# Four row maxima in an attention kernel, taken by sign clearing and halving

## The chip, the cores and the metric

The kernel runs on one core of a Trainium2 chip. The metric is the device time of one execution in microseconds (us), as the median of several runs. A core has five engines that each work through an instruction list of their own: PE (TensorE, matrix products), ACT (ScalarE), DVE (VectorE), POOL (GpSimd) and SP (SyncE, which here only issues transfers). An engine takes its instructions strictly in order, and a semaphore wait at the head of a list holds all that is behind it.

## The reference

```python
x = A_x                                                       # (1, 2048, 512), bf16
g = sigmoid((x * gate_w).sum(-1, keepdims=True))
# a: attention, 32 heads of 16 channels
qkv = (x @ wqkv).reshape(B, S, 3, 32, 16).transpose(2, 0, 3, 1, 4)
p = softmax(einsum("bhqd,bhkd->bhqk", q, k) * 16 ** -0.5, axis=-1)
a = einsum("bhqk,bhkd->bhqd", p, v) ... @ wo
# b: a feed-forward block, F = 1792
b = (silu(x @ w_gate) * (x @ w_up)) @ w_down
return g * a + (1 - g) * b
```

The exponentials of the softmax are kept in range by a bound that needs, for each head and channel, the largest magnitude of the keys over all 2048 positions. That maximum is what the change computes in another way.

## The kernel before, in words

The attention is cut into 32 units (4 blocks of 512 queries by 8 groups of 4 heads), and a unit into 16 tiles of 128 keys. For each tile PE multiplies keys with queries into PSUM (tiles `s_t` and `d_t`). The `s_t` scores become exponentials on ACT (`e_t<-s_t`, 1024 columns for each instruction). The `d_t` scores are a share that ACT has no time for: DVE takes them out of PSUM with one multiply-add into a 16-bit pattern (`c_t<-d_t`), and from this pattern DVE and POOL make shifted copies (`c_t<-c_t`; in some tiles the home of the pattern is named `kaug` or `wd_t`), which PE sums up with the values (`o_ps<-c_t,vaug`), as it does with `e_t`.

The order of the work is settled while the kernel is built. A planner runs through the program with a price for each instruction, keeps the planned time of each engine, and writes one fixed order for every engine. The projections of keys, queries and values (`kp`, `qp`, `vp`) and the feed-forward block (`gu`, `dps`, `ops`) are put between the scores, in small pieces, and share three PSUM banks with the `d_t` tiles (`m_tile`, L396): a new tile goes into the bank whose old one DVE has copied out.

POOL gets part of the copies as strips of columns. `g_now` (L1063) looks at what DVE has queued next that is not "wide" (L340; the wide ones are the fast copies and products between SBUF tiles), and `strip` (L1021) cuts a strip for POOL that fits into just that time. `beside` (L1040) makes the strip wait for DVE's last wide instruction. DVE's eviction of a PSUM tile is not wide in this sense, and neither is the step that is changed here, which is entered with a planned cost of 2.46 us (`later(2.46, top, ...)`, L1529). The change leaves this entry, and so the planned order, as it was.

The step itself is `k_bound(b)` (L517), called four times, for b = 0 to 3. Its input `kst[b]` holds 128 rows (8 heads by 16 channels) of 2048 keys in bf16; it lies in the tile `on` for b = 0, 2 and 3 and in `bblk` for b = 1, so the four show in the profile as `kb<-on` and `kb<-bblk`. `kb` is a 128x4 column tile; `k_rows` (L520) uses its column later (`kbt<-on,kb`) and sends the result into `kaug` with eight transfers on the SP queue. `mt` (128 x 14 x 512) holds the feed-forward block's hidden values; its parts 10 to 13 (2048 columns) serve the first unit as scratch (L1345) and are free from then until the feed-forward block fills them. All DVE and POOL instructions go through one helper, so the profile gives line L206 for each of them; all matrix products have L194, all activations L197.

Of the kernel before, what the change touches and what calls it, by code (L numbers as in the profile page):

```python
# [9 lines left out]
ALU = mybir.AluOpType  # L10
AX = mybir.AxisListType
BF16 = mybir.dt.bfloat16
F32 = mybir.dt.float32
U16 = mybir.dt.uint16
# [94 lines left out]
def kernel(  # L109
# [15 lines left out]
    S, D = x.shape  # L125
# [82 lines left out]
    vec = Ordered(nc.vector)  # L208
# [23 lines left out]
    for c0 in (D, 0):  # L232
        queue.dma_start(out=wqk[:, :, c0 + 64:c0 + D],
                          in_=A_wqkv[:, c0 + 64:c0 + D].rearrange("(dc p) c -> p dc c", p=P))
# [18 lines left out]
    mt = big.tile([P, FC, QBW], BF16, name="mt")  # L253
# [54 lines left out]
    kb = const.tile([P, NB], F32, name="kb")  # L308
# [87 lines left out]
    def m_tile(name, ride=None):  # L396
        while m_ready() is None:
            stuck()
        i = min((i for i in range(3) if banks[i] is not None), key=lambda i: banks[i])
        if ride is None:  # L400
            plan.pe = max(plan.pe, banks[i])
        else:
            ride.append(max(plan.pe - ROUND, banks[i]) + ROUND)
            plan.pe = max(plan.pe, ride[0])
        banks[i] = None
        held[i] = ps_m[i].tile([P, QBW], F32, tag=f"m{i}", name=name)
        return held[i]
# [88 lines left out]
    kst = {}  # L496
# [18 lines left out]
                       lambda p: later(0.6, lambda: end(tb, p)))  # L515

    def k_bound(b):  # L517
        vec.tensor_reduce(out=kb[:, b:b + 1], in_=kst[b][:, :], axis=AX.X, op=ALU.max, apply_absolute_value=True)

    def k_rows(b):  # L520

# [69 lines left out]
    def q_pieces(qb, b):  # L591
        def landed(p):
            me = plan.chain
            later(0.6, lambda: end(p, me), key=("q", b))

        def rows(t, r):
            for hh in range(8):
                gg, j = hh // 4, hh % 4
                if (b, gg) != (0, 0):
                    queue.dma_start(out=get_q(qb, 2 * b + gg)[32 * j + r:32 * j + r + DH, j % 2, :],  # L600
                                      in_=t[DH * hh:DH * (hh + 1), :])

        def end(p, me):
            qst = work.tile([P, QBW], BF16, tag="qst", name="qst")
            vec.tensor_copy(out=qst[:, :], in_=p[:, :])
            m_free(p, plan.dve)
            rows(qst, 0)

            aq = work.tile([P, QBW], BF16, tag="aq", name="aq")

            def mag():
                vec.tensor_scalar(out=aq[:, :].bitcast(U16), in0=qst[:, :].bitcast(U16), scalar1=0x8000, scalar2=None,
                                  op0=ALU.bitwise_or)
                rows(aq, DH)
            plan.chain = me
            later(0.21, mag, plan.dve, ("q", b))
        return columns(DC, "qp", lambda dc: wqk[:, dc, P * b:P * (b + 1)],
                       lambda dc: xT[:, dc, qb * QBW:(qb + 1) * QBW], landed)
# [3 lines left out]
    def q0_pieces(qb):  # L622

        st = {}

        def landed(p):
            st["p"] = p
            later(0.6, mag, key=("aq", qb))
            later(0.21, clear, key=("aq", qb))

        def mag():
            vec.tensor_copy(out=mt[:, 5, :], in_=st["p"][:, :])

        def clear():
            vec.tensor_scalar(out=mt[:, 5, :].bitcast(U16), in0=mt[:, 5, :].bitcast(U16), scalar1=0x7FFF, scalar2=None,
                              op0=ALU.bitwise_and)
            st["at"] = plan.dve + 0.12

        def bound():
            bound_add(st["p"], kneg0, mt[:, 5, :])  # L640
            spend("C", 1, st["at"])
            variants(st["p"], q0[qb], work.tile([P, QBW], BF16, tag="qst", name="qst")[:, :], note=q0_notes.setdefault(qb, []))
        return (columns(DC, "qp", lambda dc: wpad[0][:, dc, :], lambda dc: xT[:, dc, qb * QBW:(qb + 1) * QBW], landed),
                [(1, bound, False)], lambda: st["at"] <= plan.pe)
# [646 lines left out]
    def last_rows(t):  # L1291
        cs = slice(t * P, (t + 1) * P)
        return lambda i: ((onc[QB - 1][:, i, cs], wo_t[:, i, :]) if i < NB - 1 else
                          (osbs[UNITS - 2][:, cs], wo_l[:, 0, :]) if i == NB - 1 else (ident[:, :], bblk[:, t, :]))
# [71 lines left out]
    for i0, i1, h in ((0, TQ, fore), (TQ, FT, aft)):  # L1366
        for dc in (DC - 1, DC - 2):
            spare_s = dc < DC - 1 and i0
            p = ps_s.tile([P, 2 * QBW], F32, tag="s", name="tp") if spare_s else m_tile("tp")
# [14 lines left out]
    for i, dc in [(0, dc) for dc in arrived[:3]] + [(1, dc) for dc in arrived] + [(0, arrived[3])]:  # L1384
        p, h = kps[i]
# [19 lines left out]
    for v in range(2):  # L1405
        for i, h in enumerate(halves):
            if i > v:
                act(out=q0a[:, v, h], in_=qps[i][:, 0:HQ], func=ACT.Copy, scale=vsel[:, v:v + 1])
            else:
                vec.tensor_scalar(out=q0a[:, v, h], in0=qps[i][:, 0:HQ], scalar1=vsel[:, v:v + 1], scalar2=None,  # L1410
                                  op0=ALU.mult)
# [92 lines left out]
    for qb in range(1, QB):  # L1504
        d = qb * KT
        q, bd, hold = q0_pieces(qb)
        q = pace.add(q, 0, d - 13, second)
# [4 lines left out]
    for qb in range(QB):  # L1512
        for b in range(NB):
            d = UNIT.index((qb, max(2 * b, 1))) * KT
            after = []
            if qb == 0:
                ks = []
                for tb in range(QB):
                    prev = [pace.add(k_pieces(b, tb), 0, d - 40 + tb, prev)]
                    ks += prev  # L1520

                def bnd(b=b):
                    me = plan.chain

                    def top():
                        k_bound(b)
                        plan.chain = me
                        later(0.21, lambda: k_rows(b), plan.dve, ("k", b))
                    later(2.46, top, key=("k", b))  # L1529
                after = prev = [pace.add([(0.2, bnd, False)], 0, d - 34, ks)]  # L1530

            if b == 0:
                rel = UNIT.index((qb - 1, 2)) * KT + 1 if qb else 0
            elif b == 1:
                rel = UNIT.index((qb - 1, 6)) * KT + 1 if qb else 0
            else:
                rel = UNIT.index((qb, 2 * b - 2)) * KT + 1 if (qb, b) != (0, 2) else UNIT.index((0, 2)) * KT + 1
            q = pace.add(q_pieces(qb, b), rel, d - QLEAD, after)
            need.setdefault(d - 12, []).append(q)
            for g in {max(2 * b, 1), 2 * b + 1}:  # L1540
                q_of[UNIT.index((qb, g))] = q
# [440 lines left out]
    while steps:  # L1982
# [14 lines left out]
        if rest and not (best and best[0] <= plan.pe) and (best is None or best[1] != ("v", 2 * KF - 1)) and max(plan.pe, al_at(rest[0][0])) + 0.12 <= min(lim, 1e8):  # L1997
# [3 lines left out]
            w, r = last_rows(tq)(i)  # L2001
# [55 lines left out]
```

## Time and profile before

| | |
|---|---|
| time before | 742.08 us, median of 3 runs (741.69 to 742.15) |
| profiled execution, its own time | 742.09 us |
| its span, first to last instruction | 740.4 us |
| busy time | PE 721.8, DVE 715.5, ACT 728.4, POOL 299.6 us |
| the four maxima (`kb<-on`, `kb<-bblk`) | 2270, 2276, 2270 and 2286 ns; starts 62.6, 93.6, 122.6 and 169.4 us |
| granted TensorE clock | 0.999 |

What lies around the span is 1.7 us. A row of the timeline gives start, duration, engine, line, operation, the tile written, the tiles read, and the shape; a release is shown in brackets where the engine sat idle before. A duration includes the time in which an instruction waits inside the engine, and an instruction can start a little before the one ahead of it has ended, so start-to-start distances say more than durations.

### The profile page before, as it was taken

Reading aid. Unit: us, or ns where it says so; the run is one execution under the profiler, and the core shown is the slowest. Engines: PE = TensorE matmul, PEld = TensorE weight load, DVE = VectorE, ACT = ScalarE, POOL = GpSimd, SP = SyncE. Lnnn points to the kernel's source line nnn. Section 1 sums busy time; section 2 is a strip of 40 time slices with the busy share of each in tenths; the row PEclk is TensorE's granted clock in tenths of the full one; section 3 lists DMA queues with packets and bytes.
Section 4 is the critical chain, followed back from the end, with each engine's and each line's share of the span. In section 5 each row is a group of like instructions: output and inputs, shape, how many; then the busy total and the mean of one; then the engine's idle time right before and its main releaser. Section 6 shows DMA issues by size and latency. Waiting matters only on the chain.

```text
span 740.4 us, 23142 instructions
## 1 busy us (share of the span) xinstructions
PE 721.8 (97%) x9296; PEld 213.6 (29%) x9296; DVE 715.5 (97%) x1223; ACT 728.4 (98%) x828; POOL 299.6 (40%) x370
## 2 busy tenths in 40 slices
PE   8999999999999999999999999999999999999997
PEld 3323222232222222322222222222222222222223
DVE  5999999999999999999999999999999999999995
ACT  7999999999999999999999999999999999999996
POOL 4044242234453336345444225544445255343441
PEclk9999999999999999999999999999999999999999
DMA  9001233355210012320200041302001231200001
GB/s 223 14 2 29 56 62 62 63 141 101 68 44 13 17 42 68 72 48 11 58 17 24 15 107 33 80 21 60 18 12 29 64 80 44 46 19 14 20 26 36
DMA packets 93523, 36.29 MB, mean 49 GB/s; under 512 B 76448, under 2 KB 92968, under 8 KB 93416
## 3 DMA queue, kind: packets, MB, share of 16 engines
q1 hardware_dynamic: 91688, 34.49, 20.0%
q8 instruction: 72, 1.18, 0.7%
q10 hardware_dynamic: 1728, 0.33, 0.2%
q14 instruction: 35, 0.29, 0.1%
HBM read 21.42 MB, written 2.35 MB: 32 GB/s over the span
## 4 chain that ended last, share of the span: by engine, by line
PE 59%; ACT 27%; issue 6%; DVE 6%; DMA 2%; ACTq 0%; DVEq 0%
ACT e_t L197 24%; PE s_t L194 21%; PE o_ps L194 17%; PE gu L194 7%; PE ops L194 6%; DVE c_t L206 3%; ACT th L197 2%; PE qp L194 2%; PE vp L194 2%; PE dps L194 1%; PE kp L194 1%; DVE mt L206 1%; DMA wqk<-in_A_wqkv_dram 1%; DVE kaug L206 1%; DMA rb<-in_A_wqkv_dram 1%
## 5 line engine op out<-in xcount | busy, mean ns | idle before, releaser
L197 ACT ACTIVATE e_t<-s_t 128x1024 bf16<-128x1024 f32 x754 | 704.1, 1098 | 0.6 <-PE s_t L194 0.2
L206 DVE TENSOR_SCALAR c_t<-d_t 128x512 uint16<-128x512 f32 x468 | 307.2, 681 | 3.4 <-PE d_t L194 2.7
L194 PE MATMUL s_t<-qx,kaug 32*128 32x512 bf16 (+2 forms) x1208 | 233.4, 383 | 9.6 <-ACT e_t L197 8.4
L206 POOL TENSOR_SCALAR c_t<-c_t 128x352 uint16<-128x352 uint16 (+19 forms) x210 | 149.0, 710 | 210.1 <-DVE c_t L206 141.5
L194 PEld LDWEIGHTS <-kaug 32*128 32x128 bf16 (+1 forms) x2056 | 80.6, 91 | 311.5 <-issue 308.3
L194 PE MATMUL d_t<-qx,kaug 32*128 32x512 bf16 x440 | 150.2, 384 | 0.0
L194 PE MATMUL o_ps<-e_t,vaug 128*32 128x512 bf16 (+2 forms) x1608 | 148.5, 372 | 0.0
L194 PE MATMUL o_ps<-c_t,vaug 128*32 128x512 bf16 (+2 forms) x1388 | 123.8, 372 | 0.2
L206 DVE TENSOR_SCALAR c_t<-c_t 128x2048 uint16<-128x2048 uint16 (+8 forms) x185 | 116.5, 641 | 0.5
L206 POOL TENSOR_TENSOR c_t<-c_t 128x480 bf16<-128x480 bf16 (+8 forms) x53 | 65.2, 1241 | 101.7 <-DVE c_t L206 69.9
L194 PEld LDWEIGHTS <-vaug 128*32 128x32 bf16 x3236 | 67.1, 95 | 104.7 <-issue 92.4
L194 PE MATMUL gu<-xT,wg 128*32 128x512 bf16 x896 | 72.1, 384 | 0.0
L194 PE MATMUL gu<-xT,wu 128*32 128x512 bf16 x896 | 66.5, 382 | 0.3 <-DVE kaug L206 0.2
L194 PE MATMUL ops<-wd_t,mt 128*32 128x512 bf16 x672 | 55.9, 382 | 0.0
L206 DVE TENSOR_TENSOR c_t<-c_t 128x1568 bf16<-128x1568 bf16 (+8 forms) x50 | 46.8, 937 | 0.0
L206 DVE SCALAR_TENSOR_TENSOR gs<-th,gu 128x512 bf16<-128x512 bf16 x56 | 38.0, 678 | 2.0 <-ACT th L197 1.9
L206 DVE TENSOR_SCALAR kaug<-d_t 128x512 uint16<-128x512 f32 x60 | 39.6, 682 | 0.0
L206 DVE SCALAR_TENSOR_TENSOR mt<-gs,gu 128x512 bf16<-128x512 bf16 x56 | 37.9, 677 | 0.5 <-PE gu L194 0.5
L197 ACT ACTIVATE th<-gu 128x512 bf16<-128x512 f32 x56 | 37.9, 677 | 0.0
L194 PE MATMUL s_t<-q,kaug 32*128 32x512 bf16 (+1 forms) x184 | 35.8, 385 | 1.0 <-ACT e_t L197 0.9
L194 PEld LDWEIGHTS <-mt 128*32 128x32 bf16 (+1 forms) x1058 | 24.6, 95 | 27.2 <-issue 21.4
L206 POOL TENSOR_SCALAR c_t<-kaug 128x1088 uint16<-128x1088 uint16 (+15 forms) x21 | 18.4, 875 | 26.0 <-DVE c_t L206 12.7
(151 smaller groups left out, 561.0 us busy)
## 6 DMA issues: line engine op xcount, KB each, us to landing
wg<-in_B_w_gate_dram SPq DMA_DIRECT2D x56, 128.0 KB
wu<-in_B_w_up_dram SPq DMA_DIRECT2D x56, 128.0 KB
on<-osb SPq DMA_DIRECT2D x120, 16.0 KB
rb<-rr SPq DMA_DIRECT2D x15, 128.0 KB
kaug<-kbt SPq DMA_DIRECT2D x28, 64.0 KB
wd_t<-in_B_w_down_dram SPq DMA_DIRECT2D x7, 256.0 KB
qx<-qst SPq DMA_DIRECT2D x96, 16.0 KB
qx<-aq SPq DMA_DIRECT2D x96, 16.0 KB
```

The costliest lines, as they stand in the source:

```text
L194: return ordered(nc.tensor.matmul(*args, **kw))
L197: ordered(nc.scalar.activation(*args, **kw))
L206: return lambda *a, **kw: ordered(f(*a, **kw))
```

## The change

Instead of one reduction with absolute value over 2048 columns, the new step clears the sign bits of all 2048 columns into `mt`'s parts 10 to 13, takes the maximum of the first half with the second three times (1024, 512 and 256 columns are left), and reduces the last 256 columns. It runs on DVE, at the same place in DVE's list. Each of the five instructions reads what the one ahead has written and waits for it by semaphore. The instruction lists of PE, ACT, POOL and SP are the same as before.

```diff
     def k_bound(b):
-        vec.tensor_reduce(out=kb[:, b:b + 1], in_=kst[b][:, :], axis=AX.X, op=ALU.max, apply_absolute_value=True)
+
+        m = mt[:, 10:14, :].rearrange("p a q -> p (a q)")
+        vec.tensor_scalar(out=m.bitcast(U16), in0=kst[b][:, :].bitcast(U16), scalar1=0x7FFF, scalar2=None,
+                          op0=ALU.bitwise_and)
+        for w in (S // 2, S // 4, S // 8):
+            vec.tensor_tensor(out=m[:, 0:w], in0=m[:, 0:w], in1=m[:, w:2 * w], op=ALU.max)
+        vec.tensor_reduce(out=kb[:, b:b + 1], in_=m[:, 0:S // 8], axis=AX.X, op=ALU.max)
```

## The prediction

> **What bounds the kernel now.** I read the page first, then busy time by stage, then the groups of DVE by shape, then the timeline of DVE and POOL around the four maxima. The page:
>
> ```profile
> PE 721.8 (97%) x9296; PEld 213.6 (29%) x9296; DVE 715.5 (97%) x1223; ACT 728.4 (98%) x828; POOL 299.6 (40%) x370
> PE 59%; ACT 27%; issue 6%; DVE 6%; DMA 2%; ACTq 0%; DVEq 0%
> ```
>
> Three engines are nearly full and POOL is not. Busy time by stage (length, then PE, PEld, DVE, ACT, POOL) for the stages that hold the four maxima and for the rest:
>
> ```profile
> 60.00:90.00 30.00, 29.93 (x389) 8.88 (x381) 29.67 (x56) 29.96 (x34) 8.94 (x11) 1.00 0.25 50
> 120.00:165.00 45.00, 44.43 (x584) 13.44 (x576) 43.02 (x67) 45.00 (x54) 13.19 (x18) 1.00 0.43 97
> 200.00:700.00 500.00, 491.73 (x6352) 140.53 (x6348) 497.64 (x822) 499.87 (x566) 216.53 (x259) 1.00 0.17 40
> ```
>
> ACT has 0.13 us of idle time in the last 500 us. So ACT sets the end: time that ACT loses at one of the maxima is not made up later, and time gained on DVE alone shortens nothing beyond what ACT was waiting for, which is next to nothing. The question for each of the four places is only how late it makes ACT.
>
> **The step's own time.** The rows that price it are the groups of DVE by shape (count | busy us, mean ns of one):
>
> ```profile
> L206 DVE TENSOR_SCALAR c_t<-c_t 128x2048 uint16<-128x2048 uint16 x162 | 110.1, 684 | 0.5
> ...
> L206 DVE TENSOR_REDUCE kb<-on 128x1 f32<-128x2048 bf16 x3 | 6.8, 2275 | 0.0
> ...
> L206 DVE TENSOR_TENSOR on<-on,rb 128x512 bf16<-128x512 bf16 x4 | 1.7, 416 | 0.0
> L206 DVE TENSOR_TENSOR c_t<-c_t 128x1088 bf16<-128x1088 bf16 x2 | 1.4, 714 | 0.0
> ...
> L206 DVE TENSOR_REDUCE kpart<-kp 128x1 f32<-128x256 f32 x2 | 0.8, 425 | 0.9 <-PE kp L194 0.9
> L206 DVE TENSOR_TENSOR c_t<-c_t 128x896 bf16<-128x896 bf16 x1 | 0.6, 615 | 0.0
> L206 DVE TENSOR_TENSOR c_t<-c_t 128x192 bf16<-128x192 bf16 x1 | 0.2, 249 | 0.0
> ```
>
> Removed: one reduction of 2.27 us at each place. Added: the sign clearing, 0.68 (same shape as the 684 ns row); a maximum over 1024 columns, 0.68 (between 896 and 1088); over 512, 0.42; over 256, 0.28 (between 192 and 512); a reduction of 256 columns, 0.41 (the row with 425 reads fp32 from PSUM, the new one bf16 from SBUF, so I take a little less). The sum of durations is 2.47 us. How they follow each other matters as much:
>
> ```profile
> 62.62 2.27 DVE L206 TENSOR_REDUCE kb<-on 128x1 f32<-128x2048 bf16 x1
> 64.81 0.14 DVE L206 TENSOR_SCALAR ge<-vp 128x1 f32<-128x1 f32 x1
> 64.87 0.61 DVE L206 CAST vaug<-vp 128x448 bf16<-128x448 f32 x1
> ...
> 167.00 0.25 DVE L206 RECIPROCAL gval<-omg 128x16 f32<-128x16 f32 x1
> 167.29 0.18 DVE L206 TENSOR_TENSOR omg<-ge,gval 128x16 f32<-128x16 f32 x1
> ```
>
> An instruction that does not need the one ahead starts 0.08 us before that one ends (62.62 + 2.27 = 64.89, the next at 64.81). One that does need it starts 0.04 after (167.25, 167.29). All four joints in the new chain are of the second kind. Without any disturbance the next work starts after 2.47 + 4 x 0.04 - 0.08 = 2.55 us instead of 2.19: 0.36 us later at each place, 1.4 us over all four. So the change is already a small loss to DVE on paper.
>
> **What POOL does at that moment.** The planner has cut POOL's strips so that they run beside the reduction. These are the strips that meet the four reductions (at 62.62, 93.59, 122.63, 169.43), in that order:
>
> ```profile
> 62.20 0.51 POOL L206 TENSOR_SCALAR c_t<-c_t 128x384 uint16<-128x384 uint16 x1
> 62.78 1.34 POOL L206 TENSOR_SCALAR c_t<-c_t 128x1376 uint16<-128x1376 uint16 x1
> ...
> 93.15 2.13 POOL L206 TENSOR_TENSOR c_t<-c_t 128x1024 bf16<-128x1024 bf16 x1 [0.67 <-DVE c_t L206]
> 93.59 2.28 DVE L206 TENSOR_REDUCE kb<-bblk 128x1 f32<-128x2048 bf16 x1
> ...
> 122.63 2.27 DVE L206 TENSOR_REDUCE kb<-on 128x1 f32<-128x2048 bf16 x1
> 122.79 1.90 POOL L206 TENSOR_SCALAR c_t<-c_t 128x2048 uint16<-128x2048 uint16 x1 [10.29 <-DVE c_t L206]
> 124.76 0.96 POOL L206 TENSOR_SCALAR c_t<-c_t 128x928 uint16<-128x928 uint16 x1
> ...
> 168.95 0.59 POOL L206 TENSOR_SCALAR c_t<-c_t 128x480 uint16<-128x480 uint16 x1
> 169.43 2.29 DVE L206 TENSOR_REDUCE kb<-on 128x1 f32<-128x2048 bf16 x1
> 169.62 1.68 POOL L206 TENSOR_SCALAR c_t<-c_t 128x1792 uint16<-128x1792 uint16 x1
> ...
> 171.36 0.40 POOL L206 TENSOR_SCALAR c_t<-c_t 128x256 uint16<-128x256 uint16 x1
> ```
>
> The reduction takes its 2.27 to 2.29 us with strips beside it at all four places: it neither waits for POOL nor holds it up. The new instructions belong to the other kind. What these do when a strip is running shows here, where the plan had slipped:
>
> ```profile
> 104.95 1.09 POOL L206 TENSOR_TENSOR c_t<-c_t 128x480 bf16<-128x480 bf16 x1 [5.01 <-DVE c_t L206]
> 105.57 1.31 DVE L206 TENSOR_TENSOR c_t<-c_t 128x1568 bf16<-128x1568 bf16 x1
> ...
> 126.36 0.54 POOL L206 TENSOR_SCALAR c_t<-c_t 128x416 uint16<-128x416 uint16 x1
> 126.61 0.43 DVE L206 TENSOR_SCALAR kbt<-on,kb 128x512 bf16<-128x512 bf16 x1
> ...
> 163.52 0.96 DVE L206 TENSOR_TENSOR kaug<-c_t,kaug 128x1568 bf16<-128x1568 bf16 x1
> ```
>
> The same 1568-column product takes 0.96 us where the strip ends at once and 1.31 where the strip goes on until 106.04; it ends 0.84 after the strip. The 512-column copy ends 0.14 after its strip. So such an instruction stands still until the strip is over, and then needs its own duration less some 0.13. By this row the sign clearing (of the kind of the copy) ends 0.55 after a strip that blocks it, the maxima (of the kind of the product) 0.54, 0.28 and 0.14 after.
>
> [...]
>
> What no row shows is the other order: a strip that becomes ready while such a DVE instruction runs, and who goes first at the next joint. Strips follow each other in 0.06 us (62.71, 62.78), while a dependent DVE instruction starts 0.04 after its source and needs some 0.13 more before it is past the blocked part, 0.17 in all. [...]
>
> **The sum, strips first.** Place 1: clearing 62.62 to 63.30; the 1376 strip then runs to 64.64; maxima end at 65.18, 65.64, 65.96; reduction 66.41; next work at 66.33 instead of 64.81: 1.52 late. Place 2: the strip holds until 95.28; 95.83, 96.55, 97.01, 97.33, 97.78; next at 97.70 instead of 95.79: 1.91 late. Place 3: clearing to 123.31, strip to 125.21, maximum 125.75, 928 strip to 126.71, maximum 126.99, and a third strip of the length of the first row (0.51) to 127.50, maximum 127.64, reduction 128.09: 3.2 late. Place 4: clearing 170.11, strip 171.79, maximum 172.33, the 0.40 strip to 172.73, 173.01, 173.33, 173.78: 2.1 late. Together 8.7 us on DVE. A strip that waits may have its start-up behind it; the six strips that wait, at up to 0.2 each (384 columns cost 0.51, 1376 cost 1.34, so 0.19 is fixed), would give back 1.2 at most. I take 8.1.
>
> What of it reaches ACT is less by the cushions:
>
> ```profile
> 65.60 0.39 PE L194 MATMUL s_t<-on,kaug 64*128 64x512 bf16 x2
> 65.92 0.56 PE L194 MATMUL vp<-rb,xT 128*32 128x449 bf16 x8
> ...
> 66.19 1.19 ACT L197 ACTIVATE e_t<-s_t 128x1024 bf16<-128x1024 f32 x1
> ...
> 125.42 0.68 DVE L206 TENSOR_SCALAR wd_t<-d_t 128x512 uint16<-128x512 f32 x1
> ...
> 126.16 0.38 PE L194 MATMUL d_t<-qx,kaug 32*128 32x512 bf16 x1
> ```
>
> After place 1 the `vaug` copy ends at 65.48 and PE reuses that bank at 65.92: 0.44. After place 3 the eviction ends at 126.10 and PE's next `d_t` in that bank starts at 126.16: 0.06. Scores end at 65.99 and ACT takes them at 66.19: 0.20. PE takes its list in order, so when it waits for a bank, the next scores wait too. With about 0.3 for the bank and 0.2 for ACT at each place, four places keep 2.0 back, and DVE's idle time in the third stage (45.00 - 43.02) hides perhaps another 0.3. 8.1 - 2.3 = 5.8. On the profiled execution's 742.09 (the median of the runs is 742.08) that gives 747.9; as the cushions may be met more than once on the way, I say 747.7.
>
> What waits behind the chain on DVE: the evictions named, then `kbt` and its eight transfers on SP, later by the same 1.5 to 3.2 us. Their keys belong to a unit that starts tens of us later, and weights on that queue are ordered three chains ahead, so I cost the SP queue at nothing; its cover is that lead. The writes to `mt` cost no wait: its parts are free then, and the feed-forward block fills them on DVE itself.
>
> **The rivals.** [...]
>
> [...]
>
> (2) Half of it is swallowed: idle DVE time of 2 us in the third stage and larger cushions than the ones I looked at. +1.6 to +3.5, about 744.7. [...] (4) Only the chain's own 1.4 counts, as strips and chain miss each other, and cushions swallow half: +0.7, 742.8. Against it: place 2's strip starts 0.44 us ahead of the chain. (5) Not slower: the joints cost nothing, as between independent instructions, and no strip blocks. Then a place takes 2.47 - 5 x 0.08 = 2.07 instead of 2.19, -0.12 each: 741.6 at best, since ACT has nothing to give. It decides for itself only if joints start early, which the 167.29 row contradicts.
>
> [...]
>
> **How the numbers follow.** Strips first 0.50, rival 1 0.15, rival 2 0.13, rival 3 0.07, rival 4 0.09, rival 5 0.04, and 0.02 for a gain that I can't name. About 0.2% (1.5 us) is what a measurement of this kernel can tell from no change. Rivals 4 and 5 lie within it, 0.13; slower 0.85; faster 0.02. The range for 8 in 10 runs from the lower half of rival 2, 743.7, to 750.3, above the strips-first sum without any cushion given back twice; rivals 3, 4 and 5 are left out.
>
> **What would show it.** After the change, the clearing at place 2 should last about 2.2 us instead of 0.68 and end 0.55 after the strip; at places 1, 3 and 4 the first maximum should last 1.5 to 2.4 us, and the strips start or end later by about 0.6. PE should show waits for DVE's `vaug`, `wd_t` or `gs` that it does not have now, and ACT's idle time should grow by the loss. It would be wrong if all five instructions keep their short durations, or if ACT's idle time stays as it is.

## The result and the profile after

The changed kernel takes 748.25 us (median of 4 runs, 747.87 to 749.89) against 742.05 (4 runs, 741.69 to 742.15): a ratio of 1.0087, with a 95% interval of 1.0075 to 1.0099. The profiled execution is the one of 747.87 us; its span of 746.2 us is 5.8 longer than before. Of the experiments below, one execution of `late_small`, the one that was profiled, took 910.35 us at a granted clock of 0.655; its ratio leaves it out, and that kernel has no row among the shifts.

The page of the changed kernel, busy time and chain:

```profile
PE 724.0 (97%) x9296; PEld 214.2 (29%) x9296; DVE 722.0 (97%) x1239; ACT 729.4 (98%) x828; POOL 301.5 (40%) x370
PE 57%; ACT 22%; DVE 14%; issue 6%; DMA 1%; SPq 1%; ACTq 0%; DVEq 0%
```

The chain that ended last runs through DVE for 14% of the span where it was 6%: DVE was late and now holds the others. Busy time by stage shows where. The first two stretches hold the same work as the stretches 60 to 90 and 120 to 165 of before (columns as there: length, PE, PEld, DVE, ACT, POOL):

```profile
60.51:91.54 31.03, 30.20 (x389) 8.80 (x381) 30.70 (x60) 30.24 (x34) 9.32 (x11) 1.00 0.24 48
122.65:170.08 47.43, 44.71 (x584) 13.35 (x576) 45.56 (x71) 45.22 (x54) 13.95 (x18) 1.00 0.41 92
200.00:700.00 500.00, 491.54 (x6352) 140.76 (x6340) 497.89 (x823) 499.88 (x567) 216.49 (x259) 1.00 0.17 40
```

The same 34 activations now take 31.03 us instead of 30.00, with ACT idle for 0.79; the same 54 take 47.43 instead of 45.00, with ACT idle for 2.21 where it had none. The last 500 us are as full as before, so next to nothing is made up there. The staircase shows it sharply: the same activations in the timeline of ACT, of the kernel before

```profile
9.72 0.47 ACT L197 ACTIVATE mt<-qp,vsel 128x256 bf16<-128x256 f32 x1 [0.54 <-PE qp L194]
83.01 1.94 ACT L197 ACTIVATE e_t<-s_t 128x1024 bf16<-128x1024 f32 x2
123.61 0.66 ACT L197 ACTIVATE th<-gu 128x512 bf16<-128x512 f32 x1
158.60 0.69 ACT L197 ACTIVATE th<-gu 128x512 bf16<-128x512 f32 x1
192.70 0.73 ACT L197 ACTIVATE th<-gu 128x512 bf16<-128x512 f32 x1
734.89 0.69 ACT L197 ACTIVATE mt<-a_l_a,gval 128x512 bf16<-128x512 f32 x1 [1.40 <-PE a_l_a L194]
```

and of the kernel after:

```profile
10.24 0.47 ACT L197 ACTIVATE mt<-qp,vsel 128x256 bf16<-128x256 f32 x1 [0.17 <-PE qp L194]
84.55 1.94 ACT L197 ACTIVATE e_t<-s_t 128x1024 bf16<-128x1024 f32 x2 [0.22 <-PE d_t L194]
126.26 0.66 ACT L197 ACTIVATE th<-gu 128x512 bf16<-128x512 f32 x1
163.68 0.69 ACT L197 ACTIVATE th<-gu 128x512 bf16<-128x512 f32 x1
198.74 0.70 ACT L197 ACTIVATE th<-gu 128x512 bf16<-128x512 f32 x1
740.78 0.69 ACT L197 ACTIVATE mt<-a_l_a,gval 128x512 bf16<-128x512 f32 x1 [1.40 <-PE a_l_a L194]
```

The rows are 0.52, 1.54, 2.65, 5.08, 6.04 and 5.89 us later than before. The 0.52 lies ahead of the first of the four places: it is a difference between two executions' start-up, not of the change (over the experiments below the same quantity goes from -0.31 to +0.54). The four places add 1.02, 1.11, 2.43 and 0.96, and 0.15 is given back later: 5.37 in all.

### The profile page after: what moved, and what is told of

Its sections match the earlier page's. It is cut to its first block, busy times and chain, and to the rows that moved or that the text cites. A ratio compares the mean times of both kernels' runs of the same rounds, so it can differ in the third digit from the quotient of the medians.

```text
span 746.2 us, 23159 instructions
## 1 busy us (share of the span) xinstructions
PE 724.0 (97%) x9296; PEld 214.2 (29%) x9296; DVE 722.0 (97%) x1239; ACT 729.4 (98%) x828; POOL 301.5 (40%) x370
## 3 DMA queue, kind: packets, MB, share of 16 engines
q8 instruction: 72, 1.18, 0.6%
## 4 chain that ended last, share of the span: by engine, by line
PE 57%; ACT 22%; DVE 14%; issue 6%; DMA 1%; SPq 1%; ACTq 0%; DVEq 0%
PE s_t L194 19%; ACT e_t L197 19%; PE o_ps L194 17%; PE gu L194 7%; DVE c_t L206 7%; PE ops L194 6%; PE qp L194 2%; ACT th L197 2%; DVE mt L206 2%; PE dps L194 1%; PE vp L194 1%; DVE on L206 1%; DVE wd_t L206 1%; PE kp L194 1%; DVE gs L206 1%
## 5 line engine op out<-in xcount | busy, mean ns | idle before, releaser
L206 POOL TENSOR_SCALAR c_t<-c_t 128x352 uint16<-128x352 uint16 (+19 forms) x210 | 150.8, 718 | 211.8 <-DVE c_t L206 141.4
```

Source lines behind the costliest of these rows:

```text
L206: return lambda *a, **kw: ordered(f(*a, **kw))
```

## Inside the four steps

The timelines of DVE and POOL at place 3 after the change, with PE's and ACT's rows behind it:

```profile
125.27 0.69 DVE L206 TENSOR_SCALAR mt<-on 128x2048 uint16<-128x2048 uint16 x1
125.44 2.27 POOL L206 TENSOR_SCALAR c_t<-c_t 128x2048 uint16<-128x2048 uint16 x1 [10.29 <-DVE c_t L206]
125.99 2.26 DVE L206 TENSOR_TENSOR mt<-mt 128x1024 bf16<-128x1024 bf16 x1
127.79 1.28 POOL L206 TENSOR_SCALAR c_t<-c_t 128x928 uint16<-128x928 uint16 x1
128.28 1.06 DVE L206 TENSOR_TENSOR mt<-mt 128x512 bf16<-128x512 bf16 x1
129.13 0.58 POOL L206 TENSOR_SCALAR c_t<-c_t 128x384 uint16<-128x384 uint16 x1
129.38 0.47 DVE L206 TENSOR_TENSOR mt<-mt 128x256 bf16<-128x256 bf16 x1
129.89 0.42 DVE L206 TENSOR_REDUCE kb<-mt 128x1 f32<-128x256 bf16 x1
130.22 0.68 DVE L206 SCALAR_TENSOR_TENSOR gs<-th,gu 128x512 bf16<-128x512 bf16 x1
...
130.95 0.40 PE L194 MATMUL gu<-xT,wg 128*32 128x512 bf16 x4 [2.14 <-DVE gs L206]
...
131.78 1.02 ACT L197 ACTIVATE e_t<-s_t 128x1024 bf16<-128x1024 f32 x1 [2.11 <-PE s_t L194]
```

Read it as a zip: at each of the first three joints of the chain the next strip goes in. The clearing ends at 125.95 and the 2048 strip, in its engine since 125.44, runs until 127.71; the first maximum waits inside its engine and ends at 128.25, 0.54 behind the strip. The 928 strip ends at 129.07 and the 512 maximum 0.27 behind it; the 384 strip at 129.71 and the 256 maximum 0.14 behind it. The next strip (129.77 to 130.31) meets only the reduction, which keeps its 0.42. The next DVE work, `gs`, starts 4.95 us after the step began, where it was 2.19. PE waits 2.14 for `gs`, and ACT 2.11 for the scores behind it in PE's list.

At place 2 the order is the other one, and the strip meets the clearing itself. POOL and DVE there, and then DVE and POOL at place 1, whose last row is the next work on DVE:

```profile
94.69 2.13 POOL L206 TENSOR_TENSOR c_t<-c_t 128x1024 bf16<-128x1024 bf16 x1 [0.67 <-DVE c_t L206]
95.13 2.24 DVE L206 TENSOR_SCALAR mt<-bblk 128x2048 uint16<-128x2048 uint16 x1
...
63.12 0.68 DVE L206 TENSOR_SCALAR mt<-on 128x2048 uint16<-128x2048 uint16 x1
63.29 1.71 POOL L206 TENSOR_SCALAR c_t<-c_t 128x1376 uint16<-128x1376 uint16 x1
63.84 1.70 DVE L206 TENSOR_TENSOR mt<-mt 128x1024 bf16<-128x1024 bf16 x1
...
66.69 0.15 DVE L206 TENSOR_SCALAR ge<-vp 128x1 f32<-128x1 f32 x1
```

The clearing takes 2.24 us instead of 0.68 and ends 0.55 after its strip (97.37 against 96.82). Who waits, for PE and for ACT (total us, times, longest):

```profile
PE gu L194 <- DVE gs L206: 2.6, 2, 2.1
PE vp L194 <- DVE vaug L206: 1.7, 2, 0.9
...
ACT e_t L197 <- PE s_t L194: 4.4, 6, 2.1
```

The first two waits did not exist before, and the third was much smaller:

```profile
ACT e_t L197 <- PE s_t L194: 0.2, 1, 0.2
```

It is 4.4 now and not 5.4 because 747 of the 754 exponentials of the old kernel start before the activation ahead of them has ended, by 0.18 us in the median, and that overlap goes first: the one that waits at place 3 started 0.22 before that end in the kernel before, and now starts 2.11 after it.

## The experiments

The strips theory is the prediction's likeliest case: strips go first, DVE gets late, and DVE's lateness less the cushions is the loss. Against it stood mainly the chain's own length (rival 4) and late strips (rival 1, where DVE goes first at every joint). A diff that shows the old reduction is against the kernel before; one that shows parts of the chain, or leaves the reduction to three of the places, is against the changed kernel. The shifts below are those of the six ACT rows above, against the kernel before: at the start, behind places 1, 2, 3 and 4, at the end.

| kernel | start | 1 | 2 | 3 | 4 | end |
|---|---|---|---|---|---|---|
| after | +0.52 | +1.54 | +2.65 | +5.08 | +6.04 | +5.89 |
| late DVE | +0.54 | +1.56 | +2.68 | +5.11 | +5.93 | +5.74 |
| one halving | +0.23 | +1.26 | +2.38 | +4.01 | +4.91 | +4.92 |
| place 2 alone | -0.02 | -0.02 | +1.08 | +1.08 | +1.08 | +0.92 |
| place 3 alone | -0.31 | -0.32 | -0.32 | +2.11 | +2.11 | +1.96 |
| place 3 alone, second profile | -0.30 | -0.31 | -0.33 | +3.35 | +3.35 | +3.25 |
| place 3 alone, third profile | -0.10 | -0.11 | -0.12 | +2.31 | +2.31 | +2.19 |
| short step | +0.46 | +0.45 | +0.43 | +0.42 | +0.42 | +0.40 |

**A small lateness.** The old reduction, with another over 160 columns ahead of it.

```diff
     def k_bound(b):
+        vec.tensor_reduce(out=kb[:, b:b + 1], in_=kst[b][:, 0:160], axis=AX.X, op=ALU.max, apply_absolute_value=True)
         vec.tensor_reduce(out=kb[:, b:b + 1], in_=kst[b][:, :], axis=AX.X, op=ALU.max, apply_absolute_value=True)
```

> The step before (one reduction) with a second reduction of 160 columns ahead of it, which it waits for: no instruction in it can be blocked by a strip, and the step is 0.35 us longer (0.04 + 0.31), as the new chain is when nothing disturbs it. Strips theory (the loss comes from strips that POOL runs in the joints of the chain): 0.35 of lateness lies within the cushions of 0.3 and 0.2, so 742.0 to 742.9. Rival own length (the chain's 0.36 us does the harm, multiplied by waits down the line): 745 to 748.

Measured: 741.69 us against 742.03, ratio 0.9995 (0.9986 to 1.0005), 0.3 under the expected range. The estimated 0.35 us at each place (a reduction over 160 columns takes 305 ns in the short step below, and a joint 0.04), about what the chain is longer by itself, costs nothing that can be measured: the cushions hold it. The chain's own length is not the cause.

**The same lateness without collisions.** Additional reductions, sized to make DVE as late as the chain did, and no instruction that can collide with a strip.

```diff
+        for n in ((1152,), (1664,), (1216, 1088), (1536,))[b]:
+            vec.tensor_reduce(out=kb[:, b:b + 1], in_=kst[b][:, 0:n], axis=AX.X, op=ALU.max, apply_absolute_value=True)
         vec.tensor_reduce(out=kb[:, b:b + 1], in_=kst[b][:, :], axis=AX.X, op=ALU.max, apply_absolute_value=True)
```

> The step before with extra reductions ahead of it that it waits for, sized so that DVE is as late after each of the four steps as in the changed kernel (1.38, 1.92, 2.76 and 1.78 us), while no strip is held up. Strips theory, by way of a late DVE: ACT loses at each place the lateness less about 0.5, in all 5.5 to 6.0: 747.3 to 748.2. Rival late strips (the harm is that POOL's strips end late and PE waits for the copies): only DVE's share is left, 743 to 745.

Measured: 748.75 us, ratio 1.0092 (1.0075 to 1.0109): the whole loss. That is 0.55 over the expected range; the three executions without a trace ran at a mean clock of 0.995 to 0.997, and the profiled one, at 0.999, has a span of 746.2 us like the changed kernel's. Its timelines of DVE and POOL at places 1 and 3 (the rows of DVE that say x2 and x3 are the reductions of one step together):

```profile
63.15 3.65 DVE L206 TENSOR_REDUCE kb<-on 128x1 f32<-128x1152 bf16 x2
63.33 1.34 POOL L206 TENSOR_SCALAR c_t<-c_t 128x1376 uint16<-128x1376 uint16 x1
...
66.73 0.15 DVE L206 TENSOR_SCALAR ge<-vp 128x1 f32<-128x1 f32 x1
...
125.30 5.04 DVE L206 TENSOR_REDUCE kb<-on 128x1 f32<-128x1216 bf16 x3
125.45 1.90 POOL L206 TENSOR_SCALAR c_t<-c_t 128x2048 uint16<-128x2048 uint16 x1 [10.28 <-DVE c_t L206]
...
130.26 0.68 DVE L206 SCALAR_TENSOR_TENSOR gs<-th,gu 128x512 bf16<-128x512 bf16 x1
```

The strips start and run as in the kernel before (1.34 and 1.90 us), DVE's next work comes 3.58 and 4.96 after the step's start (3.57 and 4.95 in the changed kernel), and the staircase is the same within 0.03 up to place 3. So DVE's lateness is enough by itself for the whole loss, and strips that come late add nothing that can be seen. PE's longest wait for `gs` is 2.3 us, as against 2.1.

**One place at a time.** The chain at place 2 alone, and at place 3 alone (there with `(2,)`); the other three places keep the reduction.

```diff
+        if b not in (1,):
+            vec.tensor_reduce(out=kb[:, b:b + 1], in_=kst[b][:, :], axis=AX.X, op=ALU.max, apply_absolute_value=True)
+            return
```

> The new chain at the second place alone (93.6 us), the reduction at the other three. The strip there starts ahead of the chain, so only the sign clearing is blocked (2.2 us) and no strip is held up. Strips theory: DVE 1.93 late, ACT 1.2 to 1.5 late, 743.2 to 743.6, and none of it comes back. Rival own length: a quarter of the whole or less, and the same as at any other place, 742.3 to 743.6 with the first instruction at 0.68 us.

Measured: 743.01 us, ratio 1.0013 (1.0003 to 1.0022), 0.2 under the range. The step in the staircase is 1.10, as in the full change (1.11), and 0.16 comes back.

> The new chain at the third place alone (122.6 us), the reduction at the other three. Strips theory: strips of 2048, 928 and 384 columns get in at three joints, DVE 2.76 late, ACT 2.2 to 2.5 late, 744.2 to 744.6. Rival own length: the same as for the second place alone.

Measured: 745.62 us, ratio 1.005 (1.0033 to 1.0067): over the range by 1.0. The profiled execution, 743.96, has the step of 2.43 and lies 0.2 under the range, but five others lie at 745.17 to 748.81. Ordered by the mean clock that TensorE was granted they fall in line: 743.96 at 1.000, four between 745.17 and 746.19 at 0.997, 748.81 at 0.993. Two more profiles of the same kernel were meant to show what happens in such an execution.

> The kernel with the new chain at the third place alone once more, for its profile: its runs went from 743.96 (granted clock 1.0) over 745 to 746 (0.997) to 748.81 (0.993), more than the 2.0 to 2.3 us that ACT loses at the place in the first profile. Clock theory: PE's wait of 2.1 us at the place lowers the granted clock for some us behind it in some executions; a run with 0.997 shows a stage of 10 to 20 us after 130 us below 0.95, and ACT loses 1 to 2 us more there. Rival: the scatter comes from elsewhere (transfers at the start or the end), and the clock is 1.00 in all stages between 20 and 720 us.

> As the look before, a second execution: by the clock theory the step at the place is the same 2.0 to 2.3 us in both, and what goes beyond it follows the clock of the stage behind the place.

Measured: 745.24 us at a clock of 0.997, and 744.54 at 0.999 (the kernel before beside them 742.45 at 1.000). The clock theory held, though the stage of lower clock is shorter than it expected. Busy time by stage around place 3, in the second profile of this kernel and then in the third; the number behind the five engines is the granted clock:

```profile
124.63:128.04 3.41, 1.27 (x18) 0.38 (x13) 3.31 (x6) 2.05 (x3) 2.49 (x4) 1.00 0.49 81
128.04:131.45 3.41, 3.41 (x26) 0.52 (x25) 3.23 (x6) 1.71 (x2) 0.46 (x1) 0.50 0.60 119
```

```profile
123.78:127.19 3.41, 2.26 (x28) 0.73 (x25) 3.31 (x4) 3.11 (x4) 3.21 (x4) 1.00 0.57 96
127.19:130.60 3.41, 2.42 (x28) 0.63 (x27) 3.41 (x7) 1.50 (x2) 0.81 (x2) 1.00 0.59 120
```

PE waits 2.1 us for `gs` in both. Behind that wait the second profile has half the clock for exactly 3.41 us, and the third has the full clock; the staircase's step is 3.68 in the one and 2.43 in the other. So a wait of PE can cost a second time, by 1.25 us here. The clock that is missing is half of 3.41, 1.7 us.

Each trace records when its clock changed, and the stretches between lie on a grid of 3.41 us whose offset differs from one execution to the next: the full clock begins 5.28 us behind the first instruction in the kernel before and 7.11 in the changed one, and holds for 733.87 and 737.28 us, 215.0 and 216.0 times 3.413. The rows above are cut along that grid. In the second profile the whole wait fell into one stretch (PE busy for 1.27, idle for 2.14), and the next stretch had half the clock; in the third it was split over two (idle for 1.15 and 0.99). The other traces fit: the first profile of this kernel, with 1.47 and 0.67, and the changed kernel, with 1.18 and 0.96, kept the full clock, while the two kernels of another plan below had 3.20 and 2.48 us idle in one stretch and half the clock behind it (a mean of 0.91 and 0.83 from 160 to 180 us). Between 1.47 and 2.14 idle of 3.41, no run here tells what happens.

**A step that is shorter than any real one.** The reduction over the first 160 columns only; the other 1888 are left out.

```diff
-        vec.tensor_reduce(out=kb[:, b:b + 1], in_=kst[b][:, :], axis=AX.X, op=ALU.max, apply_absolute_value=True)
+        vec.tensor_reduce(out=kb[:, b:b + 1], in_=kst[b][:, 0:160], axis=AX.X, op=ALU.max, apply_absolute_value=True)
```

> The step before, with the reduction over the first 160 columns only (the other 1888 are left out, so the bound comes from fewer keys): DVE is free 1.9 to 2.0 us earlier at each of the four places, 7.8 us in all, with everything else as before. It is the most that any faster form of this step could give. ACT-sets-the-end theory: nothing or next to nothing, 741.3 to 742.2. Rival DVE sets the end: up to 734 to 738.

Measured: 742.34 us against 742.08, ratio 1.0002 (0.9992 to 1.0011), 0.1 over the expected range. The step itself is some 2 us shorter at each place (the group of DVE by shape):

```profile
L206 DVE TENSOR_REDUCE kb<-on 128x1 f32<-128x160 bf16 x3 | 0.9, 305 | 0.0
```

and the shift stays flat through all four places. DVE's next work starts only 1.74, 1.40, 0.52 and 1.07 us earlier, as it now waits for PE or ACT at places 2, 3 and 4. No form of this step, however fast, could have gained anything in this order of the work: ACT sets the end, and it does not wait for DVE in the kernel before.

**No strip planned beside the step.** One price more in the list of those that count as wide, so that the planner cuts no strip beside the step; once with the old reduction, once with the new chain.

```diff
-    PASSES = (0.87, 1.4, 1.7)
+    PASSES = (0.87, 1.4, 1.7, 2.46)
```

> The step before (one reduction), but entered in the planner as wide, so that no strip of POOL is planned beside it. The planner then writes another order for all that follows, so the time itself says little (742 to 750); it is the base for the next kernel.

Measured: 759.75 us, ratio 1.0235 (1.0219 to 1.025), outside the expectation: the edit changes the whole plan behind it, which gets worse by 17.7 us (PE there waits 4.3 us for one weight transfer), so this kernel doesn't tell what strips beside the step are worth.

> The new chain in the order of the kernel before this one: the same lists, no strip planned beside the step. Strips theory: the five instructions have their short durations (0.68, 0.68, 0.42, 0.28, 0.41), each place takes 0.36 us longer, and the time is 0 to 1.5 us above the kernel before this one. Rival (the halved maxima cost what they cost whatever POOL does): 5 to 7 us above it.

Measured: 759.95 us, 0.2 above the same plan with the reduction. On a plan this much slower the difference says little of the path; the durations say more, since almost no strip is in the way (one ends 0.16 after the step's start at place 1 and one 0.07 at place 3; groups of DVE by shape):

```profile
L206 DVE TENSOR_TENSOR mt<-mt 128x1024 bf16<-128x1024 bf16 x4 | 2.8, 692 | 0.1
L206 DVE TENSOR_SCALAR mt<-on 128x2048 uint16<-128x2048 uint16 x3 | 2.1, 694 | 0.0
L206 DVE TENSOR_TENSOR mt<-mt 128x512 bf16<-128x512 bf16 x4 | 1.7, 425 | 0.1
L206 DVE TENSOR_REDUCE kb<-mt 128x1 f32<-128x256 bf16 x4 | 1.7, 420 | 0.1
L206 DVE TENSOR_TENSOR mt<-mt 128x256 bf16<-128x256 bf16 x4 | 1.2, 292 | 0.1
```

From the step's start to the next work it takes 2.57 to 2.59 us at the four places, where the reduction takes 2.19 or 2.20 in the kernel with the same plan.

**Fewer joints.** The clearing, one maximum, and a reduction over 1024 columns.

```diff
-        for w in (S // 2, S // 4, S // 8):
-            vec.tensor_tensor(out=m[:, 0:w], in0=m[:, 0:w], in1=m[:, w:2 * w], op=ALU.max)
-        vec.tensor_reduce(out=kb[:, b:b + 1], in_=m[:, 0:S // 8], axis=AX.X, op=ALU.max)
+        vec.tensor_tensor(out=m[:, 0:S // 2], in0=m[:, 0:S // 2], in1=m[:, S // 2:S], op=ALU.max)
+        vec.tensor_reduce(out=kb[:, b:b + 1], in_=m[:, 0:S // 2], axis=AX.X, op=ALU.max)
```

> Sign clearing, one maximum of the halves, then a reduction over 1024 columns (1.21 us), in the order of the changed kernel: two instructions that a strip can block instead of four. Strips theory: places 1, 2 and 4 as in the changed kernel within 0.1 us, place 3 0.9 us better, since the strips of 928 and 384 columns no longer get in: 747.0 to 747.7, 0.5 to 1.2 below the changed kernel. Rival own length: the chain is 0.1 longer at each place, so the same as the changed kernel or 0.3 slower, 748.2 to 748.6.

Measured: 747.1 us, ratio 1.0067 (1.0052 to 1.0082), inside the range of the strips theory. DVE and POOL at its place 3:

```profile
125.72 2.26 DVE L206 TENSOR_TENSOR mt<-mt 128x1024 bf16<-128x1024 bf16 x1
127.52 1.28 POOL L206 TENSOR_SCALAR c_t<-c_t 128x928 uint16<-128x928 uint16 x1
128.01 1.22 DVE L206 TENSOR_REDUCE kb<-mt 128x1 f32<-128x1024 bf16 x1
129.15 0.68 DVE L206 SCALAR_TENSOR_TENSOR gs<-th,gu 128x512 bf16<-128x512 bf16 x1
```

The first maximum is held as before (2.26 us). The reduction behind it reads half of the columns in 1.22 us and passes the second strip (127.52 to 128.80) as if it were not there. The step in the staircase is 1.63 at place 3 instead of 2.43, and unchanged at places 1 and 2 (1.03 and 1.12), where no second strip comes.

The reverse test, the chain in the original order with the strips left away, was not tried; what rests on the traces instead is that every held instruction ended a set time after its strip (the clearing 0.55, the maxima 0.54, 0.27 and 0.14), and that the reductions passed theirs.

## Why the prediction was right, and which terms were off

**ACT sets the end and makes up nothing.** Held: 5.52 us behind the start are there after place 4, 5.37 at the end, and the short step gains nothing.

**The chain undisturbed, 2.55 us.** By the rows without strips, 0.694 + 0.692 + 0.425 + 0.292 + 0.420 = 2.52, with four joints of 0.03 to 0.04 (129.34 to 129.38 at place 3) and the overlap of 0.08 some 2.58, and 2.57 to 2.59 was measured.

**Strips first.** Held at all four places: a strip that was running held the DVE instruction (place 2), and one that was waiting went in at the next joint (places 1, 3 and 4), as the estimate from two distances had it, 0.06 from strip to strip against 0.17 for a dependent DVE instruction. The blocked clearing at place 2 ended 0.55 after its strip, as predicted; the maxima of 1024, 512 and 256 columns ended 0.54, 0.27 and 0.14 after theirs (0.54, 0.28 and 0.14 predicted). The first maxima took 1.70, 2.26 and, at place 4, 2.04 us, within the 1.5 to 2.4 named.

**How late DVE is.** This is the term that was mis-sized: 8.7 us, cut to 8.1 for the start-up that a waiting strip may have behind it. Measured from the step's start to the next work, places 1 to 4 were late by 1.38, 1.93, 2.76 and 1.81, 7.88 in all, against 1.52, 1.91, 3.2 and 2.1. The difference is what a strip saves when it has waited. At place 1 the strip ends 1.20 after the clearing, where it takes 1.34 by itself; at place 3 the strips end 1.75, 0.82 and 0.37 after the instruction that held them, against 1.90, 0.96 and 0.51. Each strip that waited thus saves 0.14 (the rows are rounded): 1.52 - 0.14 = 1.38, 3.2 - 0.43 = 2.77, 2.1 with two strips less 0.28 = 1.82, and nothing at place 2, where none waited. Six times 0.14 is 0.85; the prediction had bounded it by 1.2 and taken half. For the same reason the first strip of a place ends only some 0.4 later, from the step's start, than beside the reduction, where 0.6 was named; the second strips of places 3 and 4 end 0.7 later.

**The cushions, 2.3.** Of DVE's 7.88, 5.52 reached ACT behind the four places: 2.36 kept back. They are not even, though: 0.36, 0.82, 0.33 and 0.85, where 0.5 for each was taken from rows of places 1 and 3; that four times 0.5 came near the total is in part luck. Another 0.15 was given back later, as the 0.2 for cushions met twice had allowed.

**The sum.** 7.88 - 2.36 - 0.15 = 5.37 where 5.6 was forecast (747.7 - 742.09). The profiled execution, 747.87, is 0.17 over the forecast, and would lie under it without the 0.52 of its start-up. The median, 748.25, is over it by 0.55, and here a term is missing: two of the four executions ran at a mean clock of 0.997 and 0.995 and took 748.53 and 749.89, and the second profile at place 3 shows how PE's new wait costs clock. That the clock fell behind these waits in just these two is argued from there, as they have no trace.

**The rivals.** (1) DVE goes first at every joint: wrong, a waiting strip went in at the next joint each time. (2) Half is swallowed: wrong by size, 2.5 of 7.88 was. (3) A maximum as slow per column as the reduction: wrong, 692 ns for 1024 columns, where the reduction over 1024 takes 1.22 us. (4) The chain's own length: wrong, that much lateness costs nothing measurable. (5) Not slower: wrong, and the short step shows that its gain would not have been there either.

## What to carry to other kernels

Before a slow instruction is replaced by several fast ones, look at what another engine runs beside it: here a reduction of 2.27 us that no strip held up gave way to five instructions of 2.52 us together, four of which a strip could hold up, with a door for POOL at each joint. Even undisturbed these took longer to the next work (2.58 against 2.19). Price the joints by rows of dependent pairs, not by durations, and the blocked time by the strips that the plan puts there. And ask first whether anything waits for the step: a step cut to a seventh of its length here gained nothing.

## What the runs showed of the hardware beyond that

Each of the six strips here that a DVE instruction held up ran on for 0.14 us less, once that one had ended, than the same strip takes beside the reduction (1.20 against 1.34, 1.75 against 1.90, 0.82 against 0.96, 0.37 against 0.51, 1.54 against 1.68 and 0.26 against 0.40). That this is start-up which it has behind it by then is a reading, not shown.

A wait of PE of 2.1 us cost granted clock in one of three profiles of the same kernel (half the clock for 3.41 us) and none in the others. On the grid of 3.41 us 2.14 idle in one stretch was followed by half the clock, 1.47 was not. Executions of that kernel scattered by 4.9 us (743.96 to 748.81) where those of the kernel before scattered by 1.5 (741.51 to 742.97); that the grid explains all of this is likely but not shown, as the executions between have no trace.
